# A fused attention and SwiGLU training step: dense heads in the weight and input products, four tail tiles taken among the last backward blocks, dy added in front of the row sums

## The chip, the cores and the metric

The kernel runs on one core of one Trainium2 chip. A core has TensorE (PE, with its weight loads listed as PEld), VectorE (DVE), ScalarE (ACT), GpSimd (POOL) and SyncE (SP), each with its own in-order queue; they wait for each other by semaphores. The metric is the device time of one execution in microseconds; the median of five runs is compared.

## The reference

The kernel computes the forward output and all six gradients of one layer: a layer norm, then attention and a SwiGLU block side by side, with a residual.

```python
S, D, H, F = 2048, 448, 16, 1792          # head size 28
xn = layernorm(x)                          # no scale, no offset
A  = softmax(q k^T * 28**-0.5) v @ wo      # q, k, v = xn @ wqkv, 16 heads
B  = (silu(xn @ w_gate) * (xn @ w_up)) @ w_down
out = x + A + B
# outputs: out, and by jax.vjp with grad_out: dx, dwqkv, dwo, dw_gate, dw_up, dw_down
```

All inputs and outputs are bf16. The last output to be finished is dx. With G the gradient at xn (a sum of the products from the SwiGLU block and from dq, dk and dv with wqkv transposed), the layer norm's backward is dx = dy + rstd * (G - mean(G) - xn * mean(G * xn)), row by row, so it needs two sums over each row of G.

## The kernel before, in words

**Heads and groups.** The 16 heads are worked in 4 groups of 4. A head has 28 columns; in SBUF each head takes 32 (HP), so that four heads fill 128 partitions and a matmul of one head can use a quarter of the array. The transposed gradients dq, dk and dv of a group are kept as 128 rows with 4 rows of padding per head: dkv (two tiles of 128 x 2048, one per head pair, each with two heads of dk and two of dv) and dqT.

**Forward.** 256 slots (slot, L598) each compute four score tiles and their exponentials; between them fillers run projections, the SwiGLU forward and backward and its weight gradients. load_wq (L209) loads the wqkv columns of a group, and POOL spreads them from 28 to 32 columns per head into wq_g. For the first group that happens at the very start, in front of the second identity matrix on POOL. store_wqT (L253) transposes wq_g by DMA and stores it to wqT_d with six DMAs for the end of the kernel.

**Backward.** NB = 512 steps: group, head pair, key chunk of 512, query chunk, query tile of 128. row (L804) puts the score and dP matmuls on PE into banks sb and db (three each), ew (L832) the exponential on ACT and the product ds on DVE. Four steps make a block: in it tr_unit (L892) transposes one ds tile on PE (the others go by DMA), kv (L904) accumulates dk and dv, and dq_unit (L936) dq. Each lags behind the rows, so after step 512 there are blocks without rows in which only these run. At the end of a key chunk, kv stores a slice of dkv to dqkvT_d; at the end of a head pair dq_unit stores dqT. Stores go through a list and are issued on POOL some steps later (store and flush, L795 and L799).

**Fillers of the backward loop.** A stream of units is cut into pieces that run between the parts of a block, one bank (genb) for all: fill_step stops when its room, measured against each unit's own estimate in ns, is used up; the last slot of a block finishes the unit. In order: the forward output (y_unit), the SwiGLU part of dx (dx_unit, 10 or 8 matmuls), then after tail_open (L1143) dc_unit (L1165), which adds dq, dk and dv of the first three groups times the transposed weights to dxg, nine matmuls of 128 rows for each of 16 tiles. Among them, once per group, dsp_unit and dsq_unit transpose dk, dv and dq back, and dwq_unit (L1007) forms the gradient of wqkv: 16 matmuls of 384 columns for each of four slices of D. The padding columns are left out when its result is cast.

**The tail.** After the loop, 16 tiles of 128 rows of dx are finished (L1294 to L1354). dx_a works a pair of tiles: PE adds the last group's products into a bank tok; for the tiles in EVEN, DVE adds them to dxg and sums the row in the same instruction (L1319); for the others PE adds dxg by an fp32 identity matmul and ACT takes the row sum (L1316). A second DVE instruction forms the sum with xn (L1322). dx_b works a tile later: DVE scales the two sums (L1329), ACT forms rstd * G minus the mean (L1332), DVE xn times its sum plus dy (L1335), and POOL (for the last tile DVE) adds the two (L1337) and SP stores. Between the pairs PE and DVE or ACT finish the last group's dwqkv (the list rest).

Of the kernel before, what the change touches and what calls it, by code (L numbers as in the profile page):

```python
# [16 lines left out]
S = 2048  # L17
D = 448
# [7 lines left out]
P = 128  # L26
SCALE = DH ** -0.5
# [6 lines left out]
EVEN = (0, 2, 4, 6, 7, 8, 9, 10, 11, 12)  # L34
# [69 lines left out]
def kernel(  # L104
# [37 lines left out]
    wqT_d = dram.tile([P, 3 * G, DP_], BF16)  # L142
    dqkvT_d = dram.tile([3 * G, P, S], BF16)
# [65 lines left out]
    def load_wq(g, eng):  # L209

        raw = wk.tile([P, 4, 3, 4 * DH], BF16, name="wraw", bufs=1)
# [6 lines left out]
        for c, (d0, dn) in enumerate(DCH):  # L218
            yield
            if c == 2 and g == 0:  # L220
                ln_rstd(0)
            r4 = raw[:dn, c].rearrange("p t (h d) -> p t h d", d=DH)
            w4 = wq[:dn, c].rearrange("p t (h r) -> p t h r", r=HP)
            POOL.tensor_copy(out=w4[:, 0:2, :, :DH], in_=r4[:, 0:2])
            POOL.tensor_copy(out=w4[:, 2, 0:2, :DH], in_=r4[:, 2, 2:4])
            POOL.tensor_copy(out=w4[:, 2, 2:4, :DH], in_=r4[:, 2, 0:2])

# [16 lines left out]
    wq_g, wq_gen = {}, {}  # L244
# [7 lines left out]

    def store_wqT(g):  # L253
        wT = wk.tile([P, 4, 3, P], BF16, name="wqT_st", bufs=1)
        w = wT[:].rearrange("p c t d -> p (c t) d")
        sp_transpose(w, wq_g[g][:].rearrange("p c t r -> p (c t r)"))
        for lo, tq, i in ((0, 0, 0), (64, 0, 0), (0, 1, 1), (64, 2, 1), (0, 2, 2), (64, 1, 2)):
            late.append((wqT_d[lo:lo + 64, 3 * g + i, :].rearrange("p (c d) -> p c d", c=4),
                         wT[lo:lo + 64, :, tq, :]))
# [539 lines left out]
    def flush(upto):  # L799
        while held and held[0][0] <= upto:  # L800
            _, o, i = held.pop(0)
            POOL.dma_start(out=o, in_=i)
# [101 lines left out]
    def kv(k):  # L904
# [16 lines left out]
        if last:  # L921
# [5 lines left out]
            if g < G - 1:  # L927
                ksl = slice(kc * 512, (kc + 1) * 512)
                store(dqkvT_d[3 * g + 1 + hp, :, ksl], dkv[g, hp][:, ksl])
# [6 lines left out]
    def dq_unit(b):  # L936
# [27 lines left out]
        if qc == 3:  # L964
            dst = dqkvT_d[3 * g].rearrange("r (a q s) -> r a q s", q=2, s=P)
            for par in range(2):
                store(dst[64 * hp:64 * hp + 64, :, par],
                      dqT[g][64 * par:64 * par + 64, hp].rearrange("r (a s) -> r a s", s=P))
            if hp == 1:
# [4 lines left out]
                stream[at:at] = [(2590, lambda c=c: dwq_unit(g, c)) for c in range(4)]  # L974

    def dsq_unit(g, hp, tag="genb"):
# [5 lines left out]
        DVE.tensor_copy(out=dsp[g][:, :, 0, 64 * hp:64 * hp + 64],  # L982
# [6 lines left out]
    def dsp_unit(g, kind, t8, tag="genb"):  # L989
# [11 lines left out]
        (ACTE.copy if tag == "rest" and t8 else DVE.tensor_copy)(out=dsp[g][:, 8 * t8:8 * t8 + 8, kind, :], in_=ps[:])  # L1001
# [5 lines left out]
    def dwq_unit(g, c, tag="genb"):  # L1007
        d0, dn = DCH[c]
        ps = (ps_b if tag == "rest" else ps_g).tile([P, 3 * P], FP32, name=tag, bufs=2 if tag == "rest" else 1)
        for t in range(NT):  # L1010
            PE.matmul(ps[:dn, :], lhsT=xn_sp[:, t, d0:d0 + dn], rhs=dsp[g][:, t].rearrange("p k r -> p (k r)"),
                      start=(t == 0), stop=(t == NT - 1))
            if t < NT - 1:
                yield 162
        o = bk.tile([P, 3, 4, DH], BF16, name="dwq_o")
        p4 = ps[:].rearrange("p (k h r) -> p k h r", k=3, r=HP)
# [8 lines left out]
        yield 162  # L1025
# [117 lines left out]
    def tail_open():  # L1143
        dxst.close()
        tw = dxs["tw"] = tlst.enter_context(tc.tile_pool(name="tw", bufs=2, reuse_waits="tile"))
        dxs["wq"] = tw.tile([P, 3 * G, D], BF16, name="wqT", bufs=1)
        drip(("dc", 0), [(dxs["wq"][:, a:a + 3, :], wqT_d[:, a:a + 3, :D]) for a in (0, 3, 6)], now + 15)
# [3 lines left out]
        for lo in (0, 64):  # L1151
            for hp in range(2):
                drip(("dc", 3), [(dxs["wqd"][lo:lo + 64, hp, :], wqT_d[64 * hp:64 * hp + 64, 3 * G - 3, :D])], NB - 20)
        drip(("dc", 3), [(dxs["wq"][:, 10:12, :], wqT_d[:, 10:12, :D])], NB - 20)
# [5 lines left out]
    def load_dc(ch):  # L1160
        dcs[ch] = dxs["tw"].tile([P, 3 * G - 3, 512], BF16, name="dc")
        drip(("dc", ch), [(dcs[ch][:, a:a + 3], dqkvT_d[a:a + 3, :, ch * 512:(ch + 1) * 512].rearrange("i p s -> p i s"))
                          for a in (0, 3, 6)], now + 16)

    def dc_unit(t):  # L1165
# [5 lines left out]
        for i in range(3 * G - 3):  # L1171
            PE.matmul(ps[:, :D], lhsT=dcs[t // 4][:, i, (t % 4) * P:(t % 4 + 1) * P], rhs=dxs["wq"][:, i, :],
                      start=(i == 0), stop=(i == 3 * G - 4))
            if i < 3 * G - 4:
# [17 lines left out]
    for t in range(NT):  # L1192
        stream.append((189 * 9, lambda t=t: dc_unit(t)))
# [25 lines left out]
    def fill_step(room):  # L1219
# [7 lines left out]
        cur = None  # L1227

    NEXT = [(1, 0), (1, 2), (3, 1), (3, 2)]
    kv_n = 0  # L1230
    for k in range(NB + 12):
# [29 lines left out]
        elif m == 1:  # L1261
            b = (k - 13) // 4
            if 0 <= b < NB // 4:
                dq_unit(b)
        elif m == 2:
# [5 lines left out]
    while stream:  # L1271
        for _ in stream.pop(0)[1]():
            pass

# [6 lines left out]
    tw, wqT = dxs["tw"], dxs["wq"]  # L1281
# [4 lines left out]
    psd, sms = {}, {}  # L1286

    g = G - 1
    both = [(dkv[g, 0], wqT[:, 3 * g + 1]), (dkv[g, 1], wqT[:, 3 * g + 2])]

    nrs = tw.tile([P, NT], FP32, name="nrs", bufs=1)
    POOL.tensor_scalar(out=nrs[:], in0=rstd[:], scalar1=-1.0 / D, scalar2=None, op0=ALU.mult)

    def dx_a(t0):  # L1294
        sm = sms[t0] = tw.tile([P, 2, 2], FP32, name="sm", bufs=4)
        for t in (t0, t0 + 1):
            pst = ps_b.tile([P, 512], FP32, name="tok", bufs=6)
            psd[t] = pst[:, :D]
        odd = [t for t in (t0, t0 + 1) if t not in EVEN]
        for t in (t0, t0 + 1):  # L1300
            for i, (l, r) in enumerate(both):
                PE.matmul(psd[t], lhsT=l[:, t * P:(t + 1) * P], rhs=r, start=(i == 0), stop=False,
                          skip_group_check=True)
            if t in odd:
# [80 lines left out]
```

The softmax here doesn't subtract the row's maximum and nothing guards it: scores larger than these inputs give would overflow.

## Time and profile before

Five runs: 1442.64, 1442.90, 1444.32, 1444.69 and 1445.22 us. The profiled execution took 1442.64 us.

| | us |
|---|---|
| median of the runs | 1444.32 |
| the profiled execution | 1442.64 |
| its span, first to last instruction | 1440.9 |
| forward, up to the first ds (start to 615.8) | 615.8 |
| backward blocks, up to the last ds of the loop | to about 1394 |
| from there to the end | about 47 |
| granted TensorE clock, mean | 0.986 |

Backward blocks of four steps, by what fills them (from the start of a block's first ds to the next):

| filling | matmuls of the unit | us per block |
|---|---|---|
| dx_unit, second third of F | 8 | 5.63 |
| dx_unit, last third | 10 | 5.69 |
| dc_unit | 9 | 5.63 |
| dwq_unit | 16 | 6.42, at the end of a key chunk up to 6.89 |

How to read the views: a window line gives the busy time of PE, PEld, DVE, ACT and POOL with the number of instructions in brackets, then the granted TensorE clock, the DMA engines' busy share and GB/s. A timeline line gives start, duration, engine, source line, operation, tiles out<-in, sizes and count, and in square brackets how long the engine stood idle before it and what ended that. In a listing by form, after the bar stand busy time, mean ns of one, and the idle time before them.

### The profile page before, as it was taken

The page shows a single profiled execution, that of the slowest core. Times are in us where ns is not written, and L with a number is a line of the kernel's source. Part 1 is how long each engine was busy: PE and PEld are TensorE (multiplying, and loading weights), DVE is VectorE, ACT ScalarE, POOL GpSimd, SP SyncE. Part 2 cuts the span into 40 slices and gives each one's busy share as a digit, 9 for nine tenths or more (in the row PEclk, how much of TensorE's full clock was granted, in tenths as well). Part 3 has the DMA queues.
Part 4 walks back from the last instruction along what each step waited for, and adds up shares of the span by engine and source line. Part 5 has one row for each costly group of instructions (what it writes and reads, how often), then busy time and mean ns, then how long its engine had stood idle before and what let it go on. Part 6 is the DMA issues. An engine that isn't in the chain of part 4 may idle for free. (4 is left out here: it accounts for less than half of the span.)

```text
span 1440.9 us, 34682 instructions
## 1 busy us (share of the span) xinstructions
PE 1328.2 (92%) x12647; PEld 541.1 (38%) x12708; DVE 1151.5 (80%) x1997; ACT 1261.1 (88%) x2193; POOL 405.9 (28%) x561
## 2 busy tenths in 40 slices
PE   5889999989999999889999989999999999999996
PEld 2333333333333333333333434433443344444343
DVE  6677757666677676588998989888989999989988
ACT  5789988988999999778988989899989999989974
POOL 6574514453344453111111112201111011010106
PEclk9999999999999999989999999999999999999998
DMA  5797857796678586799999999999999999999961
GB/s 153 177 203 179 217 129 170 175 203 155 156 163 193 141 177 137 190 226 223 218 216 216 224 210 190 213 215 231 226 169 201 203 218 216 214 195 207 192 139 60
DMA packets 681179, 271.69 MB, mean 189 GB/s; under 512 B 606424, under 2 KB 655824, under 8 KB 681008
## 3 DMA queue, kind: packets, MB, share of 16 engines
q1 hardware_dynamic: 672576, 255.35, 87.1%
q0 software_dynamic: 7024, 13.82, 4.1%
q8 instruction: 100, 1.64, 0.5%
q14 instruction: 71, 0.58, 0.1%
q10 hardware_dynamic: 1408, 0.30, 0.1%
HBM read 65.09 MB, written 60.36 MB: 87 GB/s over the span
## 5 line engine op out<-in xcount | busy, mean ns | idle before, releaser
L842 DVE TENSOR_TENSOR ds_sb<-db,e_sb 128x512 bf16<-128x512 f32 x1024 | 646.8, 684 | 53.8 <-issue 20.1
L836 ACT ACTIVATE e_sb<-sb 128x512 bf16<-128x512 f32 x1024 | 554.2, 610 | 60.2 <-PE db L820 44.2
L612 ACT ACTIVATE eT<-s_w 128x1024 bf16<-128x1024 f32 x256 | 263.6, 1030 | 45.9 <-PE s_ps L609 43.1
L614 ACT ACTIVATE eT<-s_ps 128x512 bf16<-128x512 f32 x512 | 280.0, 611 | 0.0
L820 PE MATMUL db<-kd,qd 32*128 32x512 bf16 x1024 | 235.9, 383 | 8.4 <-DVE ds_sb L842 7.5
L812 PE MATMUL sb<-kd,qd 32*128 32x512 bf16 x1024 | 210.1, 386 | 5.0 <-DMA qd<-QD_d 3.2
L961 POOL TENSOR_TENSOR dq_acc<-dq_acc,dq_st 128x256 f32<-128x256 f32 x64 | 46.3, 723 | 457.1 <-ACT dq_st L959 457.1
L919 PE MATMUL acc<-ds_sb,qd 128*32 128x512 bf16 x1024 | 160.0, 388 | 0.0
L915 PE MATMUL acc<-e_sb,qd 128*32 128x512 bf16 x1024 | 157.8, 389 | 1.4 <-DVE dw_o L528 1.4
L902 ACT COPY dsT<-db 128x1024 bf16<-128x1024 bf16 x128 | 130.0, 1016 | 14.7 <-PE db L897 14.0
L380 POOL TENSOR_TENSOR nn<-nn,ag 128x512 f32<-128x512 f32 x56 | 71.3, 1273 | 249.3 <-DVE ag L378 240.6
L609 PE MATMUL s_ps<-QQ,KK 32*128 32x512 bf16 x512 | 125.3, 384 | 4.0
L1128 PE MATMUL genb<-wguT,dau_c 128*128 128x448 bf16 x448 | 117.5, 355 | 6.3 <-ACT dq_st L959 3.9
L609 PE MATMUL s_w<-QQ,KK 32*128 32x512 bf16 x512 | 100.1, 386 | 13.2 <-ACT eT L612 10.3
L812 PEld LDWEIGHTS <-qd 32*128 32x128 bf16 x1024 | 48.2, 91 | 149.1 <-issue 139.6
L421 PE MATMUL gen<-xn_t,f_sp 128*128 128x448 bf16 x416 | 91.8, 354 | 2.6 <-DVE nn L395 1.7
L421 PEld LDWEIGHTS <-f_sp 128*128 128x128 bf16 x640 | 55.7, 98 | 75.7 <-issue 32.1
L946 PE MATMUL genb<-dsT,kd 128*32 128x256 bf16 x2048 | 79.7, 276 | 2.2 <-DVE dqT L955 0.6
L897 PE MATMUL db<-ident_bf,ds_sb 128*128 128x128 bf16 x1032 | 79.4, 220 | 1.1 <-DVE ds_sb L842 1.1
L897 PEld LDWEIGHTS <-ds_sb 128*128 128x128 bf16 x1032 | 68.2, 99 | 24.5 <-issue 5.6
L381 POOL TENSOR_TENSOR nn<-nn,tt 128x512 f32<-128x512 f32 x56 | 72.1, 1288 | 4.4
L609 PEld LDWEIGHTS <-KK 32*128 32x128 bf16 x1024 | 29.0, 91 | 115.3 <-issue 112.3
(167 smaller groups left out, 1953.2 us busy)
## 6 DMA issues: line engine op xcount, KB each, us to landing
F_d<-hda SPq DMA_DIRECT2D x56, 384.0 KB, 3.1
dau_c<-F_d SPq DMA_DIRECT2D x24, 512.0 KB, 4.4
qd<-QD_d SPq DMA_DIRECT2D x16, 512.0 KB
kd<-KD_d SPq DMA_DIRECT2D x16, 384.0 KB, 3.9
dsT<-ds_sb SPq DMA_TRANSPOSE x383, 4.5
dc<-dqkvT_d SPq DMA_DIRECT2D x12, 384.0 KB, 3.7
h_c<-F_d SPq DMA_DIRECT2D x8, 512.0 KB, 5.3
wT_d<-wT_f SPq DMA_DIRECT2D x14, 256.0 KB, 3.6
```

The costliest lines, as they stand in the source:

```text
L421: PE.matmul(ps[:, :D], lhsT=fsp[fc][:, t // 4, w, t % 4, :], rhs=rhs[:, t, :], start=(t == 0), stop=(t == NT - 1))
L609: PE.matmul(sp4[hh], lhsT=KK[g][r:r + HP, kt * P:(kt + 1) * P], rhs=QQ[g][r:r + HP, qsl], start=True, stop=True, tile_position=(r, 0))
L612: ACTE.activation(out=e2[0][:], in_=wide[:], func=ACT.Exp, scale=SCALE)
L614: ACTE.activation(out=e2[1][:, j], in_=sp4[2 + j], func=ACT.Exp, scale=SCALE)
L812: PE.matmul(s_ps[:], lhsT=qside[g, qc][r:r + HP, 0, qi * P:(qi + 1) * P], rhs=kside[g, kc][r:r + HP, 0, :], start=True, stop=True, tile_po ...
L820: PE.matmul(d_ps[:], lhsT=qside[g, qc][r:r + HP, 1, qi * P:(qi + 1) * P], rhs=kside[g, kc][r:r + HP, 1, :], start=True, stop=True, tile_po ...
L836: ACTE.activation(out=est[k][:, j], in_=sps.pop((k, j))[:], func=ACT.Exp, scale=SCALE)
L842: DVE.tensor_tensor(out=ds[:, j], in0=dps.pop((k - 1, j))[:], in1=est[k - 1][:, j], op=ALU.mult)
L897: PE.transpose(ps[:, c, :], ds[:, c // 4, (c % 4) * P:(c % 4 + 1) * P], ident_bf[:])
L902: ACTE.copy(out=o, in_=ps[:])
L915: PE.matmul(a[r:r + HP, :], lhsT=sp4[:, 1, r:r + HP], rhs=e[:, j, :], start=first, stop=last, tile_position=(0, r), skip_group_check=True)
L919: PE.matmul(a[r:r + HP, :], lhsT=sp4[:, 0, r:r + HP], rhs=ds[:, j, :], start=first, stop=last, tile_position=(0, r), skip_group_check=True)
```

## The change

It has five parts; lines that only rename are left out.

1. **Dense rows for dc_unit.** dq, dk and dv of the first three groups are stored without the padding rows, 1008 rows as 8 x 126 (crow gives each head's place), and the transposed weights come from the loaded columns themselves, which are padded with zeros to a multiple of 128. dc_unit has eight matmuls over 126 rows for nine over 128. dk and dv are stored once per head pair, in four DMAs of 28 rows, dq in four per head pair instead of two.
2. **Dense columns for dwq_unit.** 12 x 28 = 336 columns instead of 384; the moving operand skips the padding by its access pattern.
3. **Four tail tiles early.** The matmuls of tiles 0 and 1 stand behind dq_unit of block 125, their sums behind dq_unit of block 126, with the matmuls of tiles 2 and 3; they use the banks sb and db. The last stores after the loop go out on SP instead of POOL.
4. **dy in front of the sums.** For each tile DVE forms v = rstd * G + dy in dx_a, before the scaling of the sums; ACT forms u = xn * sum + sum, and dx = u + v.
5. **Who does what.** Tiles 1, 3 and 5 join EVEN; three copies of the last group move from DVE to ACT; the order of the remaining units of the last group changes; the last pair keeps its two sums in separate tiles.

```diff
@@ load_wq, store_wqT
-        raw = wk.tile([P, 4, 3, 4 * DH], BF16, name="wraw", bufs=1)
+        rawp = raws[g] = wk.tile([P, 4, 3 * P], BF16, name="wraw", bufs=1)
+        raw = rawp[:, :, :12 * DH].rearrange("p c (t n) -> p c t n", t=3)
...
+        POOL.memset(rawp[:, :, 12 * DH:], 0.0)
+        POOL.memset(rawp[64:, 3, :12 * DH], 0.0)
...
+        if g < G - 1:
+            sp_transpose(w, raws[g][:].rearrange("p c r -> p (c r)"))
+            for t in range(3):
+                a, n = 336 * g + P * t, min(P, 336 - P * t)
+                late.append((wqc_d[a:a + n, :].rearrange("p (c d) -> p c d", c=4), wT[:n, :, t, :]))
+            return
@@ flush
-            POOL.dma_start(out=o, in_=i)
+            (POOL if now < NB else SP).dma_start(out=o, in_=i)
@@ kv, dq_unit
-            if g < G - 1:
-                ksl = slice(kc * 512, (kc + 1) * 512)
-                store(dqkvT_d[3 * g + 1 + hp, :, ksl], dkv[g, hp][:, ksl])
+            if kc == 3 and g < G - 1:
+                for h in range(4):
+                    store(dqkvc_d[crow(g, 1 + hp, h), :], dkv[g, hp][HP * h:HP * h + DH, :])
...
+            for j in range(2):
+                dst = dqkvc_d[crow(g, 0, 2 * hp + j), :].rearrange("r (a q s) -> r a q s", q=2, s=P)
+                for par in range(2):
+                    r = 64 * par + HP * j
+                    store(dst[:, :, par], dqT[g][r:r + DH, hp].rearrange("r (a s) -> r a s", s=P))
@@ dwq_unit
-            PE.matmul(ps[:dn, :], lhsT=xn_sp[:, t, d0:d0 + dn], rhs=dsp[g][:, t].rearrange("p k r -> p (k r)"),
+            PE.matmul(ps[:dn].rearrange("p (a r) -> p a r", r=DH), lhsT=xn_sp[:, t, d0:d0 + dn], rhs=dsp[g][:, t].rearrange("p k (h r) -> p (k h) r", r=HP)[:, :, :DH],
...
-                yield 162
+                yield 142
@@ tail_open, load_dc, dc_unit
+        nrs = dxs["nrs"] = tw.tile([P, NT], FP32, name="nrs", bufs=1)
+        POOL.tensor_scalar(out=nrs[:], in0=rstd[:], scalar1=-1.0 / D, scalar2=None, op0=ALU.mult)
...
+        drip(("dc", ch), [(dcs[ch][:CP, a:b], src[:, a:b]) for a, b in ((0, 3), (3, 6), (6, 8))], now + 16)
...
-        for i in range(3 * G - 3):
+        for i in range(NCP):
@@ the tail, new
+    def dx_v(t):
+        ps = psd.pop(t)
+        vs[t] = kq.tile([P, 512], FP32, name="ds_sb", bufs=10)[:, :D]
...
+        DVE.scalar_tensor_tensor(out=vs[t], in0=ps, scalar=rstd[:, t:t + 1], in1=dy, op0=ALU.mult, op1=ALU.add)
...
+    def dx_a(t0):
...
+        if t0 == NT - 2:
+            dx_sm(t0)
+        for t in (t0, t0 + 1):
+            dx_v(t)
+        if t0 < NT - 2:
+            dx_sm(t0)
+
+    def dx_b(t):
+        sa, sb = sums(t, 0), sums(t, 1)
+        u = kq.tile([P, 512], FP32, name="e_sb", bufs=5)[:, :D]
+        ACTE.activation(out=u, in_=xn_sp[:, t, :], func=ACT.Identity, scale=sb, bias=sa)
+        dx = dxs["tw"].tile([P, D], BF16, name="dx", bufs=4)
+        (DVE if t == NT - 1 else POOL).tensor_tensor(out=dx[:], in0=u, in1=vs.pop(t), op=ALU.add)
+        SP.dma_start(out=out1_d[:, t, :], in_=dx[:])
@@ the loop, behind dq_unit
+            if k > NB and k < NB + 8:
...
+                if k < NB + 4:
+                    dx_mm(0)
+                else:
+                    dx_a(0)
+                    dx_mm(2)
@@ after the loop
+    ahead.update((t, tok(t)) for t in (4, 5))
+    for _ in range(4):
+        run(rest.pop(0))
+    dx_a(2)
+    at = {4: 1, 6: 1, 8: 1, 14: 1}
+    for t in range(4, NT + 2, 2):
         if t < NT:
+            dx_mm(t)
             dx_a(t)
-        for u in (t - 2, t - 1):
-            if u >= 0:
-                dx_b(u)
+        for u in range(0 if t == 4 else t - 2, t):
+            dx_b(u)
         for _ in range(at.get(t, 0)):
             run(rest.pop(0))
```

dx_mm holds the matmuls that dx_a began with before, in the same order; dx_sm is the scaling of the sums that stood in dx_b, and dx_a's row sums are unchanged. EVEN grows from (0, 2, 4, 6 to 12) to (0 to 12).

## The prediction

> **What bounds the kernel now.** I read the page's busy shares first, then busy times by window over blocks of four backward steps, then the timeline of one block and of the end.
>
> ```profile
> PE 1328.2 (92%) x12647; PEld 541.1 (38%) x12708; DVE 1151.5 (80%) x1997; ACT 1261.1 (88%) x2193; POOL 405.9 (28%) x561
> ...
> 1270.20:1276.60 6.40, 6.40 (x80) 2.85 (x76) 5.65 (x13) 5.51 (x11) 1.39 (x2) 1.00 1.07 215
> 1098.99:1104.62 5.63, 5.59 (x68) 2.17 (x69) 5.47 (x11) 5.39 (x12) 0.73 (x1) 1.00 0.99 214
> 1169.35:1175.04 5.69, 5.69 (x74) 2.34 (x67) 5.53 (x11) 5.43 (x11) 0.72 (x1) 1.00 1.08 244
> 1336.98:1342.61 5.63, 5.63 (x69) 2.24 (x69) 5.48 (x11) 5.38 (x12) 0.00 (x0) 1.00 1.17 247
> ```
>
> Three engines are nearly full, so the block decides. The windows are one block each, by the filling in them: dwq_unit (16 matmuls), dx_unit with 8, dx_unit with 10, dc_unit with 9. Eight and nine matmuls take the same 5.63 us, because VectorE is full; ten take 5.69. The dwq block takes 6.40, and there VectorE waits:
>
> ```profile
> 1267.13 0.39 PE L812 MATMUL sb<-kd,qd 32*128 32x512 bf16 x2
> ...
> 1267.50 0.50 PE L1011 MATMUL genb<-dsp,xn_t 128*128 128x384 bf16 x2
> ...
> 1268.28 1.30 PE L1011 MATMUL genb<-dsp,xn_t 128*128 128x384 bf16 x7
> ...
> 1269.51 0.39 PE L812 MATMUL sb<-kd,qd 32*128 32x512 bf16 x2
> ...
> 1269.62 0.27 DVE L1018 CAST dwq_o<-genb 128x112 bf16<-128x112 f32 x1 [0.65 <-PE genb L1011]
> ```
>
> Only the slot with nine of the sixteen matmuls (2 and 7) keeps VectorE waiting. The rows of scores ahead of it start just as VectorE frees a db bank (ds operations of about 0.64 us from 1263.82, rows at 1264.51, 1265.89, 1267.13), so the other seven lie in slack.
>
> The end:
>
> ```profile
> 1398.19 0.42 DVE L955 SCALAR_TENSOR_TENSOR dqT<-genb,dq_acc 128x256 bf16<-128x256 f32 x1 [0.80 <-PE genb L946]
> ...
> 1401.42 0.62 DVE L1319 SCALAR_TENSOR_TENSOR dxg<-tok,dxg 128x448 f32<-128x448 f32 x1 [1.59 <-PE tok L1309]
> ...
> 1433.33 1.08 DVE L1329 TENSOR_TENSOR sm<-sm,nrs 128x4 f32<-128x4 f32 x1
> 1434.52 2.04 DVE L1335 SCALAR_TENSOR_TENSOR ds_sb<-xn_t,sm,dsT 128x448 f32<-128x448 bf16 x2
> ...
> 1436.75 1.28 DVE L1337 TENSOR_TENSOR dx<-e_sb,ds_sb 128x448 bf16<-128x448 f32 x1 [0.19 <-issue]
> ```
>
> From 1401.42 to 1438.03 VectorE sets the pace with few gaps. By window it is busy only 4.75 of the 8 us before 1399. The listing by form shows whom the adds on POOL cost:
>
> ```profile
> L1322 DVE SCALAR_TENSOR_TENSOR pr<-dxg,xn_t 128x448 bf16<-128x448 f32 x10 | 8.3, 826 | 0.3
> ...
> L1322 DVE SCALAR_TENSOR_TENSOR pr<-tok,xn_t 128x448 bf16<-128x448 f32 x6 | 3.6, 618 | 0.7 <-ACT gs L1316 0.7
> ```
>
> **Dense heads.** *dwq_unit:* 336 columns for 384. Spacing of the seven matmuls is (1.30 - 0.326) / 6 = 0.162 us; by columns 0.142. Nine in the deciding slot save 9 x 0.020 = 0.18; the split becomes 2, 5, 3 and 6 under the new estimates, so again nine. Twelve units lie in the loop: **-2.2 us**. Ends: 0 if another wait takes over at once, and 16 x 0.020 x 12 = -3.9 if all count (VectorE's idle time there, 8.4 us over twelve, in the view of its line, would allow it). I take nine, since the timeline shows which are covered. The four units in the tail lie beside VectorE: 0; uncovered they would gain 4 x 16 x 0.020 = 1.3.
>
> *dc_unit:* eight matmuls for nine, 16 times. The windows say 0: VectorE covers them. Without that cover the gain would be 16 x 0.19 = 3.0.
>
> *Stores of dq, dk, dv:* POOL issues 24 of 28 rows x 4 KB for 24 of 128 KB (0.57 us each), and 24 for 12 of dqT (0.70). That is 12 x 0.70 = 8.4 us more of issuing, in batches of four: 2.3 or 2.8 us. POOL idles about 5 us in each block before its add of dq (L961, 457 us in all), which hides a batch; a y store behind one is 2.8 us late, while y has two buffers and a new one comes each 5.9 us. Uncovered, the 8.4 us would stand in full. SP issues 9 fewer stores of the transposed weights in the forward loop; the 12 dc loads stay 12 and land in 3.7 us, due 16 steps (22 us) ahead: 0.
>
> The Trainium skill, DMA: Bandwidth & Descriptors, in the section on why a DMA increments its semaphore by 16, says that a transfer is spread over the largest number up to 16 that divides its slowest dimension. By that, 126 or 28 rows use 14 engines, and a dc load of 3.7 us would land in an estimated 4.2, which moves no sum; no run here shows it yet.
>
> *load_wq:* two more memsets on POOL. Rows of 128x128 take 0.205 and 64x256 0.307, so about 0.25 and 0.35. In the first group they stand before ident_f, in a stretch where POOL is busy without a break from 9.04 to rstd at 15.64, for which VectorE waits 0.56 (L238 at 16.72); from there VectorE is full until the next projection on PE. **+0.5 us**, ends 0 and +0.65. For the other three groups POOL waits 240 us on the gates: 0.
>
> **The tail.** PE takes dx_mm(0), eight matmuls or about 1.3 us (L1302 x4 and L1309 x4), ahead of tr_unit(127) and dq_unit(126), and dx_mm(2) ahead of dq_unit(127). VectorE takes dx_a(0), seven operations, ahead of the last L955, and dx_a(2) behind it. No dx store moves ahead of the two dy loads on SP. Against the tail as it ran:
>
> - Start: L955 of dq_unit(126) ends at 1398.6 + 1.3 = 1399.9, and the first dx operation follows at once, for 1401.42: -1.5.
> - Three copies (L1001 0.69, L982 1.28 for two) go to ACT: -2.0. ACT takes four copies of 1.01 while VectorE does the first four tiles.
> - The last L955 now stands in the stretch: +0.4. Behind it wait genb, hence one rest bank, dsq and the dwq units; PE still has tile 4 ready by about 1407.4, before VectorE wants it at 1407.9.
> - Tiles 1, 3 and 5 gain a sum operation: 3 x 0.67 (1401.42 to 1402.09) = +2.0; tile 5's pr then reads SBUF beside the adds, +0.3. Six fp32 matmuls on PE go, beside VectorE.
> - Waits that go: 0.54 and 0.78 on tok, 0.67 on ACT's gs: -2.0.
> - v (new place of the L1335 work) now stands before the sums, so POOL's adds, 2.4 to 2.8 us a pair, fall on pr and on v instead of on a PSUM sum. Two v's took 1.28 alone and 2.04 beside adds. I take +0.3 for five pairs: +1.5; ends 0 and 0.6.
> - Last pair: from sm of tile 12 with the two pr's it took 7.2, less 1.28 for v12 and v13, which move = 5.9. After: ACT does two u (1.47), four casts (0.6), two u (1.4), then the 1.28 add: 4.8. -1.1.
>
> - nrs (0.27 us on POOL) moves to tail_open and waits there for the tiles of the dx pool; the next in POOL's queue is an add of dq that needs later PE work anyway: 0, and 0.3 if not. The four last dwq stores leave POOL (0.69 each, between its adds) for SP, where each waits for ACT's casts with the following dx stores behind it; the casts end before those dx tiles do: 0, or about 0.4 (one issue of SP) ahead of the last two.
>
> Sum **-2.4 us**. Ends: -4.7 if the adds cost v nothing and VectorE, not ACT, ends the last pair (0.8 sooner); +0.6 if the start gains nothing and v pays double.
>
> Total -2.2 + 0.5 - 2.4 = **-4.1 us**: the profiled execution of 1442.64 (span 1440.9, 1.7 outside it) becomes 1438.5, its span 1436.8. It was the fastest of the five; from the median 1444.32 I predict **1440.2**. Ends: 1435.7 and 1445.6.
>
> **Rivals.** (1) The dwq blocks find another wait as the dc blocks did: -1.9, 1442.4. For it: ACT is busy 5.51 of 6.40. Against: VectorE's idle 0.65 comes before its casts, straight after PE.
> (2) Both gains at their full ends, with the 0.5: -8.1, 1436.2. For it: the idle 8.4 us and a last pair free of POOL; against: the rows gated by db.
> (3) The end is held by ACT and POOL, tail 0: -1.7, 1442.6. For it: casts before the last two u's; against: POOL is busy 22 of 39 us there.
> (4) Slower: dwq's moving operand is now read in runs of 28 out of 32 elements, and no matmul of the trace reads such short runs. Nearest slow row is the fp32 matmul of 448 columns, spaced 0.92 - 0.54 = 0.38 us against 0.19 for bf16. At that rate a dwq matmul takes 0.285: 9 x 0.123 x 12 = +13.3, less 1.9: 1455.7, and 1466 if all sixteen count. It turns the sum positive from 0.162 + 1.9 / 108 = 0.180 us a matmul.
> The Trainium skill, SBUF — State Buffer, Door 1 (the DMA port swizzle), puts free striding at two or more accesses in each 16-byte line; a run of 56 bytes on a 64-byte grid keeps that, so by it rival 4 falls away. No row here shows it.
>
> **How the numbers follow.** Forecast 0.50 (own range 1438 to 1442.5), rivals 0.14, 0.18, 0.08, 0.10. Measurement tells about 0.2%, 2.9 us, from no change. Faster: most of the forecast (0.42), rival 2, a little of 1 and 3: 0.63. Slower: rival 4 and a remainder: 0.12. Same: 0.25. Range 1436 to 1444.5: rival 4 and the far tips stay out.
>
> **What would show it.** dwq blocks at 6.2 us with VectorE's wait near 0.47, and matmuls spaced 0.142; dc blocks still 5.63; first sum of tile 0 near 1399.9 - 1.7 = 1398.2; no wait before the sum of tile 4; v beside adds over 0.9 us; KK's second projection 0.5 us later at the start. A dwq spacing over 0.18 or a tail of 36 us again would make it wrong.

## The result, and the profile after

The changed kernel took 1445.17 us (median of 43 runs, 1438.93 to 1452.02), the kernel before, run beside it, 1442.90 (79 runs, 1437.29 to 1451.83). The ratio is 1.0014, 95% interval 1.0006 to 1.0023: some 2.0 us slower (0.0014 x 1443; 0.9 to 3.3), where 4.1 us less were predicted. Both kernels spread over more than 10 us, so that one profile is one draw: the profiled execution before had a span of 1440.9, the one after 1446.3.

The first view is the busy time by window over four stretches: forward, blocks 0 to 39, blocks 40 to 127, and from the last block on. The columns are start:end, length, busy PE, PEld, DVE, ACT, POOL, then the granted clock, the DMA share and GB/s. Before:

```profile
8.02:616.38 608.36, 557.04 (x3997) 215.32 (x4059) 402.70 (x709) 534.05 (x831) 272.54 (x360) 0.99 0.75 172
616.38:864.42 248.04, 229.99 (x2545) 93.93 (x2547) 222.00 (x366) 218.13 (x404) 38.36 (x62) 0.97 1.11 216
864.42:1389.01 524.59, 504.52 (x5816) 212.94 (x5817) 481.29 (x816) 484.32 (x906) 69.02 (x103) 1.00 1.09 204
1389.01:1440.90 51.89, 36.65 (x298) 18.91 (x294) 40.73 (x94) 23.34 (x55) 22.15 (x19) 0.88 0.31 83
```

The same stretches after:

```profile
8.00:620.77 612.77, 560.73 (x3998) 216.63 (x4060) 403.75 (x711) 534.55 (x831) 274.56 (x368) 0.98 0.73 171
620.77:869.20 248.43, 229.22 (x2545) 93.82 (x2547) 222.56 (x366) 218.52 (x403) 39.91 (x65) 0.97 1.12 216
869.20:1395.60 526.40, 502.36 (x5800) 211.99 (x5802) 480.81 (x815) 485.32 (x905) 73.87 (x112) 1.00 1.11 201
1395.60:1446.30 50.70, 33.23 (x292) 17.72 (x292) 43.01 (x98) 24.56 (x52) 19.64 (x15) 0.87 0.34 85
```

The first stretch ends with the first ds, which begins at 616.38 us before (not at 615.8). Of the 5.4 us between the spans, 4.4 arise in the forward loop, where the change adds two memsets a group and leaves out nine stores of weights. The blocks from the 40th on, which should have got 2.2 us shorter, took 1.8 more. The end got 1.2 shorter.

The 1.8 us are a sum of opposite parts. The twelve dwq blocks got 2.9 us shorter. Blocks 97 to 101 took 2.6 us more at a full clock, with waits of 1.4 us on a load of qd and 1.2 us on transposes of ds; the other profiles with rows stored in batches (e3, e10 and e11 below) lack this. Block 110, the first with a dc_unit, took 1.4 more, and two later dc blocks 0.35 each.

Single blocks after, in the same view: dx_unit with 8 matmuls, with 10, two with dwq_unit, two with dc_unit (blocks 114 and 115):

```profile
1096.18:1101.81 5.63, 5.58 (x68) 2.17 (x69) 5.47 (x11) 5.38 (x12) 0.73 (x1) 1.00 1.11 174
1172.18:1177.87 5.69, 5.69 (x74) 2.34 (x67) 5.52 (x11) 5.43 (x11) 0.73 (x1) 1.00 1.15 216
1269.27:1275.46 6.19, 6.19 (x80) 2.75 (x72) 5.62 (x13) 5.70 (x11) 1.00 (x2) 1.00 1.18 158
1275.46:1281.66 6.20, 6.20 (x78) 2.84 (x76) 5.63 (x13) 5.63 (x11) 1.46 (x2) 1.00 1.03 201
1319.57:1325.63 6.06, 5.83 (x68) 2.26 (x69) 5.74 (x12) 5.50 (x11) 0.00 (x0) 1.00 1.06 239
1325.63:1331.26 5.63, 5.59 (x68) 2.17 (x70) 5.47 (x10) 5.10 (x10) 0.00 (x0) 1.00 1.35 179
```

The dwq blocks take 6.20 as predicted. The dc blocks take 5.63, but one in this fence (block 114) and one more later (block 122) took 0.35 longer (6.06 for 5.71, 5.98 for 5.63). PE's part of the timeline of one dwq block:

```profile
1271.63 0.89 PE L1028 MATMUL genb<-dsp,xn_t 128*128 128x336 bf16 x5
...
1272.91 0.60 PE L1028 MATMUL genb<-dsp,xn_t 128*128 128x336 bf16 x3
...
1273.79 1.02 PE L1028 MATMUL genb<-dsp,xn_t 128*128 128x336 bf16 x6
```

Six matmuls are spaced (1.02 - 0.305) / 5 = 0.143 us, 0.305 being the length of one. By columns 0.142 were worked out, so the short runs of 28 elements cost nothing here.

The start, in POOL's timeline:

```profile
10.69 0.25 POOL L231 MEMSET wraw<- 128x192 bf16 x1
11.00 0.37 POOL L232 MEMSET wraw<- 64x336 bf16 x1
...
16.37 1.05 POOL L237 TENSOR_TENSOR rstd<-rstd,m_half 128x4 f32<-128x4 f32 x1
```

rstd stood at 15.64 before: +0.73.

The end, in DVE's timeline:

```profile
1405.03 0.61 DVE L1311 SCALAR_TENSOR_TENSOR dxg<-sb,dxg 128x448 f32<-128x448 f32 x1
...
1411.47 1.28 DVE L1288 SCALAR_TENSOR_TENSOR ds_sb<-dxg,rstd,dy 128x448 f32<-128x448 f32 x2
...
1413.74 0.63 DVE L1311 SCALAR_TENSOR_TENSOR dxg<-tok,dxg 128x448 f32<-128x448 f32 x1 [0.92 <-PE tok L1279]
...
1417.13 3.02 DVE L1288 SCALAR_TENSOR_TENSOR ds_sb<-dxg,rstd,dsT 128x448 f32<-128x448 f32 x2
...
1420.14 0.61 DVE L1311 SCALAR_TENSOR_TENSOR dxg<-tok,dxg 128x448 f32<-128x448 f32 x1
1420.79 0.62 DVE L1314 SCALAR_TENSOR_TENSOR pr<-dxg,xn_t 128x448 bf16<-128x448 f32 x1
...
1422.83 2.14 DVE L1288 SCALAR_TENSOR_TENSOR ds_sb<-dxg,rstd,dsT 128x448 f32<-128x448 f32 x2
...
1424.96 0.61 DVE L1311 SCALAR_TENSOR_TENSOR dxg<-tok,dxg 128x448 f32<-128x448 f32 x1
```

and in POOL's:

```profile
1414.10 5.56 POOL L1328 TENSOR_TENSOR dx<-e_sb,ds_sb 128x448 bf16<-128x448 f32 x4 [21.87 <-ACT e_sb L1326]
1421.20 2.68 POOL L1328 TENSOR_TENSOR dx<-e_sb,ds_sb 128x448 bf16<-128x448 f32 x2 [1.54 <-DVE dxg L1311]
```

Two v's take 1.28 us alone, 2.14 beside the adds of one pair, and 3.02 beside the four adds of the early tiles, which all come at once behind pair 4. A pair takes 4.82 (1420.14 to 1424.96), against 4.35 before (1417.25 to 1421.60):

```profile
1417.25 0.62 DVE L1319 SCALAR_TENSOR_TENSOR dxg<-tok,dxg 128x448 f32<-128x448 f32 x1
...
1421.60 0.62 DVE L1319 SCALAR_TENSOR_TENSOR dxg<-tok,dxg 128x448 f32<-128x448 f32 x1
```

Tile 4 is waited for 0.92 us. PE's transposes ahead of it wait 2.17 us for the last dq, and then run at half speed, for the clock is at 0.50 from 1409.1 to 1412.5. The same eight transposes, first after and then in e2 below: there the clock is full, PE waits as long, and VectorE does not wait for tile 4 at all:

```profile
1409.19 1.01 PE L1015 MATMUL rest<-ident_bf,dkv 128*128 128x128 bf16 x8 [2.17 <-DVE dqT L971]
1397.94 0.61 PE L998 MATMUL rest<-ident_bf,dkv 128*128 128x128 bf16 x8 [2.16 <-DVE dqT L955]
```

Last, the clock. Windows of one us at one place of the forward loop, after:

```profile
182.00:183.00 1.00, 0.25 (x2) 0.16 (x2) 1.00 (x3) 0.99 (x3) 0.15 (x1) 1.00 0.69 151
183.00:184.00 1.00, 1.00 (x6) 0.46 (x5) 0.22 (x1) 0.00 (x0) 0.47 (x1) 0.84 0.51 111
184.00:185.00 1.00, 1.00 (x7) 0.22 (x5) 0.00 (x0) 0.00 (x0) 0.00 (x0) 0.50 0.23 86
185.00:186.00 1.00, 1.00 (x7) 0.33 (x7) 0.00 (x0) 0.35 (x1) 0.00 (x0) 0.50 1.01 253
```

and the same place before, one us earlier in its span:

```profile
181.00:182.00 1.00, 0.69 (x4) 0.38 (x4) 0.79 (x2) 0.91 (x2) 0.58 (x1) 1.00 0.96 219
182.00:183.00 1.00, 1.00 (x10) 0.38 (x7) 0.00 (x0) 0.00 (x0) 0.04 (x1) 1.00 1.17 214
183.00:184.00 1.00, 1.00 (x8) 0.42 (x9) 0.00 (x0) 0.59 (x1) 0.00 (x0) 1.00 0.48 87
```

Behind a stretch in which PE stands idle (1.72 us after, 1.37 before) the granted clock falls to 0.50 for 3.4 us after and stays at 1.00 before, and what follows on the path is late by about 1 us. After has such falls at 184 and 314 us, and longer ones than before at 20 and 40; the shift of the forward slots between the two profiles grows at these places (by 1.4 and 0.95 us at the first two). The Trainium skill, TensorE: Matmul & The Clock Gate, in Part 1, says that PE runs at half rate after an idle window of 3.4 us and that the window runs free of the kernel's start. The trace agrees on the half rate (0.50 or 1.00, and means of the two where a window of the table holds both) and on the length and the free running: in both profiles the changes of the clock lie whole multiples of 3.41 us apart. It differs on the idle time: in the 3.4 us ahead of the fall at 183.7 PE was busy for half of the time and idle for 1.72 us at a stretch, so less than a whole idle window was enough. Since the windows run free, the same idle stretch can bring a fall in one execution and none in the next.

Every run lists its mean granted clock. It was 0.9791 in the changed kernel (44 executions) and 0.9822 to 0.9825 in the kernel before (means of 29 to 35 executions on each of four chips). Within the runs of the kernel before the time falls by 0.59 to 0.96 us for each 0.001 of clock, by chip (correlation -0.49 to -0.79), within the changed kernel's by 0.77 (-0.62). So 0.0032 less goes with 1.9 to 3.1 us, 2.5 by the changed kernel's own slope. This is a correlation: no run changes the clock and nothing else.

### The profile page after: what moved, and what is told of

Same layout as the page of the kernel before. It is cut to its first block, busy times and chain, and to the rows that moved or that the text cites. A ratio compares the mean times of both kernels' runs of the same rounds, so it can differ in the third digit from the quotient of the medians.

```text
span 1446.3 us, 34642 instructions
## 1 busy us (share of the span) xinstructions
PE 1325.5 (92%) x12625; PEld 540.1 (37%) x12686; DVE 1154.7 (80%) x2001; ACT 1264.2 (87%) x2190; POOL 411.8 (28%) x577
## 5 line engine op out<-in xcount | busy, mean ns | idle before, releaser
L836 PE MATMUL db<-kd,qd 32*128 32x512 bf16 x1024 | 239.8, 384 | 9.8 <-DVE ds_sb L858 8.5
```

What stands on the lines that cost most here:

```text
L836: PE.matmul(d_ps[:], lhsT=qside[g, qc][r:r + HP, 1, qi * P:(qi + 1) * P], rhs=kside[g, kc][r:r + HP, 1, :], start=True, stop=True, tile_po ...
```

## The experiments

In the traces the blocks from the 40th on repeat to 0.02 us from kernel to kernel (the dwq blocks of e1 and of the changed kernel, for instance), except where the clock falls or a transfer is late, so that small steps can be read there even where a ratio can't tell.

**Each part alone, and one taken away.** *e1_dwq*: only the dense dwq_unit.

```diff
-            PE.matmul(ps[:dn, :], ..., rhs=dsp[g][:, t].rearrange("p k r -> p (k r)"),
+            PE.matmul(ps[:dn].rearrange("p (a r) -> p a r", r=DH), ..., rhs=dsp[g][:, t].rearrange("p k (h r) -> p (k h) r", r=HP)[:, :, :DH],
```

> The kernel before with the dense dwq_unit alone (336 columns for 384). Theory rows (the dense rows of dq, dk, dv and of the weights cost about 5 us in the loop and the start, and eat a dwq gain of 2.9 and a tail gain of 1.2): 2.9 us less, ratio 0.998. Rival tail (the dwq gain is 2.9, the rows cost under 1, and the new tail is some 4 us slower than it looks): also 0.998. Rival slack (the dwq blocks get shorter but the loop gets it back elsewhere): ratio 1.000.

Ratio 0.9984 (0.9966 to 1.0002); clock 0.9825. From the start of block 40 to that of block 127 it took 521.65 us for 524.59: -2.94, all of it in the twelve dwq blocks, of which one by window:

```profile
1271.17:1277.36 6.19, 6.19 (x76) 2.84 (x76) 5.62 (x13) 5.62 (x11) 1.39 (x2) 1.00 1.06 240
```

No other of these blocks differs by more than 0.02 us, so nothing gives it back there: the rival of the slack falls.

*e2_norows*: the changed kernel with part 1 undone.

```diff
-            if kc == 3 and g < G - 1:
-                for h in range(4):
-                    store(dqkvc_d[crow(g, 1 + hp, h), :], dkv[g, hp][HP * h:HP * h + DH, :])
+            if g < G - 1:
+                ksl = slice(kc * 512, (kc + 1) * 512)
+                store(dqkvT_d[3 * g + 1 + hp, :, ksl], dkv[g, hp][:, ksl])
...
-        for i in range(NCP):
+        for i in range(3 * G - 3):
```

> The changed kernel with the dense rows undone (dq, dk, dv and weights in blocks of 128 rows again, nine matmuls in dc_unit, no two memsets); dense dwq_unit and the new tail stay. Theory rows: 2.9 + 1.2 = 4.1 us less than before, ratio 0.997, and no waits on the transposes of ds after a group's end. Rival tail: 1.1 us more, ratio 1.001. Rival slack: about 1.001, since neither dwq nor the tail pays.

0.9984 (0.9964 to 1.0004), clock 0.9818. Its point lies 0.0030 below the changed kernel, so the rows cost something, but between the two theories' numbers. The long dc blocks are gone (5.71 and 5.63).

*e3_rows*: only part 1, on the kernel before.

```diff
+            if kc == 3 and g < G - 1:
+                for h in range(4):
+                    store(dqkvc_d[crow(g, 1 + hp, h), :], dkv[g, hp][HP * h:HP * h + DH, :])
...
+        POOL.memset(rawp[:, :, 12 * DH:], 0.0)
+        POOL.memset(rawp[64:, 3, :12 * DH], 0.0)
```

> The kernel before with the dense rows alone (stores by heads of 28 rows in batches of four, eight dc matmuls, two memsets). Theory rows: 4 to 6 us more, ratio 1.0028 to 1.004, of it 0.75 at the start and the rest in the blocks after the batches of stores and at the first dc_unit. Rivals tail and slack: 0.5 to 0.8 us more, ratio 1.0005.

1.0006 (0.9987 to 1.0025), clock 0.9828: the rivals' 1.0005 fits, and the theory's 1.0028 to 1.004 lies outside, if barely. In its trace rstd stands at 16.48 and the dc blocks of 6.06 and 5.98 are there: 0.75 and 0.7 us that belong to the rows. Two more blocks (48 and 64), each with the one behind it, lose 1.2 and 1.1 us; see e8 and e9 on these.

*e4_tail*: only the new tail.

```diff
+                if k < NB + 4:
+                    dx_mm(0)
+                else:
+                    dx_a(0)
+                    dx_mm(2)
...
+        for t in (t0, t0 + 1):
+            dx_v(t)
```

> The kernel before with the new tail alone (early tiles, v ahead of the row sums, three copies on ScalarE, last stores on SP). Theory rows: 1.2 us less, ratio 0.999. Rival tail: 3 to 4 us more, ratio 1.0025. Rival slack: about 1.001.

0.9993 (0.9974 to 1.0012), clock 0.9829: the rival of a slow tail, 1.0025, falls. From its first sum to the end of its last add it takes 37.90 us against 36.60 before. Its first sum comes 4.91 us behind the start of the last ds. Before it was 7.90 in the profile, but 6.45 in e3, which has the old tail; the new tail has 4.91 here and 6.26 in e2. The clock parts them: before and in e2 it falls to 0.50 right behind the last ds (at 1394.0 before), in e3 and here it does not. One us of the stretch before and one of that in e3:

```profile
1395.00:1396.00 1.00, 1.00 (x17) 0.57 (x10) 0.19 (x1) 0.57 (x1) 0.00 (x0) 0.50 0.00 0
1399.00:1400.00 1.00, 1.00 (x29) 0.89 (x27) 0.94 (x2) 0.25 (x1) 0.00 (x0) 1.00 0.13 15
```

All 17 profiles go by this: with a fall there the first sum comes 7.85 to 7.90 us behind the last ds in the old tail and 6.21 to 6.33 in the new one, without it 6.45 and 4.90 to 4.91. So like with like the first sum gains 1.5 us, as predicted. The stretch from it to the last add gives back 0.9 to 1.5, and the last store lands 0.2 to 0.3 later. From the last ds to the end of the span it is 46.76 us in e2 for 47.34 before, with the fall, and 45.86 here for 45.78 in e3 without it: the tail is worth nothing, or a gain of half a us. Where the new tail has no fall right behind the last ds, one comes some 9 us later, at the wait ahead of tile 4.

**Mending the rows.** *e5_mend*: the changed kernel with the stores of a batch three steps apart, the first group's memsets behind the start, and the first dc loads four steps earlier.

```diff
-    def store(o, i):
-        held.append((now + 2, o, i))
+    def store(o, i, lag=2):
+        held.append((now + lag, o, i))
+        held.sort(key=lambda x: x[0])
...
-                    store(dqkvc_d[crow(g, 1 + hp, h), :], dkv[g, hp][HP * h:HP * h + DH, :])
+                    store(dqkvc_d[crow(g, 1 + hp, h), :], dkv[g, hp][HP * h:HP * h + DH, :], 2 + 3 * h)
...
-        POOL.memset(rawp[:, :, 12 * DH:], 0.0)
-        POOL.memset(rawp[64:, 3, :12 * DH], 0.0)
+        if g:
+            pad_wq(g)
...
-... for a, b in ((0, 3), (3, 6), (6, 8))], now + 16)
+... for a, b in ((0, 3), (3, 6), (6, 8))], now + (16 if ch else 12))
```

> The changed kernel with three mends of the dense rows: the four stores of a batch are let go three steps apart instead of together, the two memsets of the first group stand behind the start, and the first loads of dc fall due four steps earlier. Theory batch (a burst of four row stores holds up the transposes of ds that VectorE's operations wait for, and the first dc load comes too late): the blocks after a group's end and the first dc block lose their 1 to 4 us of waits, the blocks from the 40th on take 522.4 us as a whole against 526.4 changed and 524.6 before, the start loses 0.75, and the ratio to before is 0.998. Rival form (rows of 28 cost DMA time however they are issued): only the start and the dc block gain, 2.1 of some 5 us, ratio 1.000. Rival luck (the waits come and go between runs): ratio as the changed kernel's less 0.0005, 1.001.

0.9971 (0.9954 to 0.9988), clock 0.9807: faster than both kernels. Its profile is one of its longer executions (1442.70 us) and has 523.9 us from block 40 on where 522.4 were expected; the clock falls at blocks 64 and 96 and takes 2.2 of them; the two long dc blocks are gone. Run again on another chip as *e15_mend2*:

> The mended kernel of the fifth experiment once more, unchanged, on the chip of these runs. If its gain was the kernel's, ratio to before 0.996 to 0.999; if it was that chip's or chance, 0.999 to 1.001, as the sum of its traced parts plus the changed kernel's lower clock would make it.

0.9982 (0.9965 to 1.0000), clock 0.9802. The gain holds, if smaller: its interval ends at 1.

The three mends one by one, each on the changed kernel. *e9_spread* has only the `lag`, *e10_dcearly* only `now + (16 if ch else 12)` (and 11 for 15 at the weights), *e11_memset* only `pad_wq`.

> The changed kernel with only the four row stores of a batch let go three steps apart. Theory batch: it brings the part of the mended kernel's gain that the start and the dc loads don't explain, some 3 us of 6: ratio to before 0.9993, blocks 97 to 101 at before's times. Rival late (the dc loads and the start are the systematic cost, and waits after a group's end come by chance in every kernel): ratio as the changed kernel's, 1.001, with the waits at the first dc block and the two long dc blocks (6.06 and 5.98 us) still there.

> The changed kernel with only the first loads of dc and of the dense weights due four steps earlier. Theory late: the first dc block loses its wait (1.4 us) and the two long dc blocks are 5.7 and 5.63 us (0.7 less together): 2.1 us less, ratio to before 1.000. Theory batch: the same 2.1 us here, and the rest in the other experiment. Rival: earlier loads push transposes of ds aside, and the dwq blocks before get longer by what the dc block gains: ratio 1.0014.

> The changed kernel with only the two memsets of the first group moved behind the start. All theories: GpSimd's second rstd begins at 15.6 to 15.9 instead of 16.37, and the forward slots come 0.75 us earlier: ratio to before 1.0009. If the start is hidden after all: 1.0014.

0.9996 (0.9981 to 1.0012), 1.0003 (0.9991 to 1.0015) and 0.9996 (0.9978 to 1.0013): each below 1.0014, none apart from it. In the traces: the memsets' 0.73 us go in e11 (rstd at 15.75). The dc blocks of 6.06 and 5.98 stay in e10 and e11 and are gone in e9, e5 and e15 (5.71 and 5.63), so they hang on the stores going in a batch, by a way that the profile doesn't name: the last store of dq, dk or dv is issued at 1224.5, some 95 us ahead. The wait for the first dc loads, 1.4 us after, in the view of waits by window

```profile
PEld L1192 <- DMA dc<-dqkvc_d: 1.7, 1, 1.7
PE genb L1192 <- DMA dc<-dqkvc_d: 1.4, 1, 1.4
```

is gone in e10, but also in e11 and e3, and 0.35 of it is left in e9: it shows only where SyncE's queue happens to be late. After, the last piece was issued at 1293.15 and the unit's first matmul began at 1296.28, 3.1 us later; before at 1285.05 and 1291.77, 6.7 us. PE wanted that piece for its seventh matmul at 1298.54 and had it at 1299.93, 6.8 us behind the issue (6.2 in e9), where the loads before landed in 3.5 to 4.3. Whether the form of the rows or the queue made it slower isn't shown.

*e8_batch* batches the stores of the kernel before, with 128 rows as they were:

```diff
-            if g < G - 1:
-                ksl = slice(kc * 512, (kc + 1) * 512)
-                store(dqkvT_d[3 * g + 1 + hp, :, ksl], dkv[g, hp][:, ksl])
+            if kc == 3 and g < G - 1:
+                for c in range(4):
+                    ksl = slice(c * 512, (c + 1) * 512)
+                    store(dqkvT_d[3 * g + 1 + hp, :, ksl], dkv[g, hp][:, ksl])
```

> The kernel before with nothing but its four stores of a dk or dv held back to the end of the last key chunk and let go together: 128 rows as before, no dense row. Theory batch: waits of 1 to 3 us in the blocks after a group's end (blocks 48, 64 and 96 on), together 2 to 3 us, ratio 1.0015 to 1.002. Rival form: no such waits, ratio 1.000, blocks from the 40th on 524.6 as before.

1.0003 (0.9984 to 1.0022): no long blocks at 48, 64 or 96, but one at 80 (7.55 for 6.68). In e9 the blocks 64 and 96 are long in spite of the spread stores, and in e6 below, which has no dense rows, 48, 64 and 96. The clock tells why; e9 by windows, at block 64:

```profile
1019.00:1020.00 1.00, 0.24 (x1) 0.10 (x1) 1.00 (x3) 1.00 (x3) 0.00 (x0) 1.00 0.29 56
1020.00:1021.00 1.00, 0.94 (x10) 0.94 (x10) 1.00 (x3) 0.10 (x1) 0.00 (x0) 0.56 1.14 260
1021.00:1022.00 1.00, 1.00 (x13) 0.74 (x10) 0.27 (x2) 0.17 (x1) 0.00 (x0) 0.50 0.84 285
```

Here PE waits twice for the bank of the transposes, 0.89 and 0.82 us, in each of the 17 profiles; in eight of them the clock falls behind it and 0.9 to 1.2 us go. So the theory that a batch of stores holds up the transposes of ds falls for these blocks. Waits on those transposes there were in the changed kernel's profile, at blocks 32 to 34, right behind the batches of group 0, 4.1 us on DVE:

```profile
DVE ds_sb L858 <- DMA dsT<-ds_sb: 4.1, 3, 1.9
PE genb L962 <- DMA dsT<-ds_sb: 2.0, 2, 1.7
```

but blocks 30 to 38 are unsteady in kernels without rows too (7.60 for 5.88 at block 34 in e1).

**The tail.** *e6_adds*, on e2: the last steps of the early tiles ahead of pair 4.

```diff
+    dx_b(0)
+    dx_b(1)
     for _ in range(4):
         run(rest.pop(0))
     dx_a(2)
+    dx_b(2)
+    dx_b(3)
...
-        for u in range(0 if t == 4 else t - 2, t):
+        for u in range(4 if t == 4 else t - 2, t):
```

> The second experiment (no dense rows) with the last steps of tiles 0 to 3 put ahead of pair 4, so that GpSimd's first four adds run while VectorE does early tiles and waits, not beside pair 4's sums and v's. Theory v (v beside an add takes 1.54 us for 0.67): pair 4 falls from 6.4 to 4.8 us or less, and the stretch from the first sum to the end from 40.5 to about 39. Rival: ScalarE's steps for tiles 0 to 3 delay its four copies, dsp comes later and the end is the same or up to 2 us later. Ratio to before 0.9975 or 0.9985.

0.9975 (0.9958 to 0.9992). Pair 4 falls from 6.4 to 4.5 us with its v's at 1.28, but there is a wait of 1.61 before it, which e2 does not have:

```profile
1409.77 0.62 DVE L1293 SCALAR_TENSOR_TENSOR dxg<-tok,dxg 128x448 f32<-128x448 f32 x1 [1.61 <-PE tok L1261]
...
1413.01 1.28 DVE L1270 SCALAR_TENSOR_TENSOR ds_sb<-dxg,rstd,dsT 128x448 f32<-128x448 f32 x2
```

and the adds of tiles 0 and 1 now slow the v's of pair 2 (2.14). The stretch is 38.1 (37.45 in e2): the theory was right on pair 4, and on the end the rival's number came. But the clock is at 0.50 for 6.8 us around that wait, so how much of it the order makes and how much the clock isn't settled.

*e7_vback*, on e2: the last step as it was.

```diff
-        ACTE.activation(out=u, in_=xn_sp[:, t, :], func=ACT.Identity, scale=sb, bias=sa)
+        ACTE.activation(out=t1, in_=psd.pop(t), func=ACT.Identity, scale=rstd[:, t:t + 1], bias=sa)
+        DVE.scalar_tensor_tensor(out=t2, in0=xn_sp[:, t, :], scalar=sb, in1=dy, op0=ALU.mult, op1=ALU.add)
```

> The second experiment (no dense rows) with the last step of a tile in its old form: VectorE's second operation is xn times the sum plus dy again, behind the row sums, and ScalarE reads G; the early tiles stay. Theory v: pairs 6, 8 and 10 take 4.35 us again instead of 4.82, pair 4 also 4.4 to 5, the stretch from the first sum to the end is some 2 us shorter (38.5), less up to 1 us at the last pair. Rival (the extra sums of tiles 1, 3 and 5 and the waits are what costs): the stretch stays at 40 to 41.

0.9979 (0.9962 to 0.9997). The middle pairs take 4.35 us again, with 1.28 for the two operations; DVE's timeline from pair to pair:

```profile
1416.60 0.62 DVE L1285 SCALAR_TENSOR_TENSOR dxg<-tok,dxg 128x448 f32<-128x448 f32 x1
...
1419.76 1.27 DVE L1301 SCALAR_TENSOR_TENSOR ds_sb<-xn_t,sm,dsT 128x448 f32<-128x448 bf16 x2
1420.95 0.62 DVE L1285 SCALAR_TENSOR_TENSOR dxg<-tok,dxg 128x448 f32<-128x448 f32 x1
```

But pair 4, expected at 4.4 to 5, takes 6.78 us, for its four last operations stand beside adds too (4.23 for the four), and the last two tiles pay again (1.55 and 1.54). Tile 4 is waited for 1.02 us. The stretch is 38.0: these lose what the middle gains. The theory holds for v, not for the end.

*e12_tail2* and *e13_tail3*, on e5, mix both forms:

```diff
-        for t in (t0, t0 + 1):
-            dx_v(t)
+        if t0 >= 12:
+            for t in (t0, t0 + 1):
+                dx_v(t)
...
+    dx_mm(4)
+    dx_a(2)
+    dx_b(0)
+    dx_b(1)
     for _ in range(4):
         run(rest.pop(0))
```

and e13 besides

```diff
+            if t == 12:
+                dx_b(t - 2)
+                dx_b(t - 1)
             dx_a(t)
...
-        (DVE if t == NT - 1 else POOL).tensor_tensor(out=dx[:], ...)
+        (DVE if t in (NT - 3, NT - 1) else POOL).tensor_tensor(out=dx[:], ...)
```

> The mended kernel (fifth experiment) with another tail: v ahead of the sums only for the last four tiles, the old last step for the other twelve, tile 4's products on TensorE ahead of the transposes that wait for the last dq, and the last steps of tiles 0 and 1 ahead of ScalarE's copies. Theory v (v beside GpSimd's adds costs what the last pair gains): pairs of 4.35 us in the middle, no wait of 0.9 before tile 4, the last pair as in the changed kernel, stretch from the first sum to the last add 36 us instead of 38: ratio to before 0.996. Rival (some other engine, ScalarE or GpSimd, holds the tail at 38): ratio 0.997 as the mended kernel.

> The mended kernel with the tail of e12 and its two faults put right: the last steps of tiles 10 and 11 stand ahead of pair 12, and the add of tile 13 is on VectorE, so that GpSimd has not five adds left at the end. Theory v: middle pairs 4.35 us, last dx add some 36.5 us behind the first sum (38.1 in the changed kernel, 40 in e12), the tail from the last ds to the end 44.5 us where the first sum comes 4.9 us behind it (46.1 in the changed kernel); ratio to the mended kernel of the same chip 0.999. Rival (ScalarE or GpSimd hold the end whatever VectorE does): 38 again, ratio 1.000 to it.

e12: 0.9996 (0.9979 to 1.0013). Tile 6 comes late: DVE waits 5.62 us for it, behind a dwq unit whose 16 matmuls take 4.12 us for 2.45, as the clock falls there. Then POOL still has five adds left when DVE has done its last sums, and the end comes 48.3 us behind the last ds, 1.6 later than in e5; POOL's timeline:

```profile
1430.65 6.09 POOL L1343 TENSOR_TENSOR dx<-e_sb,ds_sb 128x448 bf16<-128x448 f32 x5 [1.97 <-DVE ds_sb L1341]
```

e13: 1.0011 (0.9996 to 1.0026), 50.3 us; against e15, beside which it ran, 1.0025 by the medians. Tile 6 comes late again, behind a dwq unit that waits for ACT's copies, after 6.8 us at half clock:

```profile
1417.53 0.62 DVE L1319 SCALAR_TENSOR_TENSOR dxg<-tok,dxg 128x448 f32<-128x448 f32 x1 [4.22 <-PE tok L1286]
```

Both miss: with DVE eased, POOL's adds and PE's order hold the end, with falls of the clock on top that the profiles don't let one take out. *e14_tail3n* has e13's tail without the rows:

> The same tail without the dense rows (on the second experiment). If the mended rows cost nothing, its ratio to before is that of e13_tail3 within 0.001; if rows of 28 cost DMA time however they are issued, it is 0.001 to 0.002 lower and its granted clock is higher.

1.0007 (0.9988 to 1.0026), clock 0.9798 against e13's 0.9782: the ratios are within 0.001, but their intervals leave room for 0.002 either way, and the clock is higher by about one error. So this does not tell what the mended rows cost.

## Why the prediction was wrong

It called the direction wrong. Its mechanisms in the loop were mostly right; two sizes (the new work of the tail and the stores) and one resource (the clock) were not.

- **dwq, -2.2.** Right: -2.94 in twelve blocks (e1), 6.20 a block, with a spacing of 0.143 in the changed kernel. The split was 2, 5, 3 and 6, as worked out; nine count, and a little more of the other seven. Rival 4 (short runs) is refuted, rival 1 too.
- **dc_unit, 0.** Right for 14 of 16 blocks; two lost 0.35 each while the stores came in batches. Its "due 16 steps (22 us) ahead: 0" was wrong as a margin: the last piece was issued only 3.1 us ahead of the unit, and landed in 6.8 us instead of 3.7, or 4.2 by the prediction's other estimate. One profile of those with batches shows 1.4 us of waiting, e9 0.35. The due step is where the plan aims, not where a full queue issues.
- **The stores, 0.** Issuing was indeed hidden by POOL: in the backward loop no other engine waits for it. What the stores did elsewhere was not costed. Undoing or mending part 1 together with its start is worth 0.0030 to 0.0043 of ratio (e2, e5 and e15 against the changed kernel), each with an interval of some 0.002 either way; of this 0.75 us at the start and 0.7 in the dc blocks are placed, the rest not.
- **load_wq, +0.5.** 0.73, just over its end of 0.65.
- **The tail, -2.4.** This is the step that failed by size. The first sum came 1.5 us sooner, as worked out, though the row that it was measured from, 1401.42, had a fall of the clock in front. "I take +0.3 for five pairs" for v beside POOL's adds was wrong. The prediction's own row, 2.04 for 1.28, made 0.76 a pair, and no reason was given for less than half of it. Three pairs pay 0.86 (2.14 for 1.28), pair 4, on which the adds of all four early tiles fall, 1.74, and tile 12 0.33: together 4.65 for 1.5. Cheaper pr's in three pairs (0.62 for 0.90) give back 0.8. "Tile 4 ready before VectorE wants it" held in e2 and e5 and failed (0.92) where the clock fell in front of it. Measured: -1.5 at the first sum, +0.9 to +1.5 in the stretch, +0.25 at the last store, so about 0. Rival 3 had a tail of 0, but for another reason, ACT and POOL holding the end.
- **The granted clock.** No step had it. The sum was made against a profile with 0.986 and carried to the median as if the clock were the kernel's own constant. It is not: the changed kernel has 0.0032 less on average, which goes with some 2.5 us.

Together -2.9 + 0.7 + 0.7 + 0 + 2.5 = +1.0, against +2.0 (0.9 to 3.3) measured. For e5 and e15 the same sum makes -2.9 + 0 + 1.2 = -1.7 and -2.9 + 0 + 1.8 = -1.1 (0.0015 and 0.0023 less clock than before on their chips), against -4.2 and -2.6 measured (intervals of 2.5 us each way); what is left there isn't settled. Nor is it settled which part lowers the clock. dwq, rows and tail alone left it (0.9825, 0.9828, 0.9829; 12 runs each, errors 0.0006 to 0.0010); dwq and tail together had 0.9818, 0.9803, 0.9818 and 0.9798, all three 0.9782 to 0.9817. No kernel was made that keeps PE busy at those places, which would be the test.

## What to carry to other kernels

Where a loop repeats, take the price of a step from the blocks and not from the total: here twelve blocks gave 2.94 us to the hundredth, while the total needed 43 runs to tell 2. Work that is moved beside a second engine's SBUF operations must be priced at the instruction it will stand beside, one by one, and the engine that is not the bound must be followed too: each mended tail found the next one (POOL's adds, PE's order). A step of preparation, such as a pad or a batch of stores, is best put where no one waits for its queue: moving them, with the loads a little earlier, stands between a loss of 2 us and a gain of 3 to 4, of which the traces place 1.5 us. And look at the granted clock of a window before its times are compared: here it parted two profiles of the same tail by 1.4 us.

## What the hardware showed that was not expected

The clock of PE falls to 0.50 for 3.4 us at fixed places of the program, behind idle stretches on PE where this was looked at (1.72 us in the forward loop; 0.89 and 0.82 us, 3.0 us apart, at a head pair's end), in one execution and not in the next. A fall costs 0.9 to 1.4 us on the path in the loops and 1.3 to 1.5 right behind the last ds. Outside the tail the clock was at 0.50 for 27.3 us before and 44.4 after in the two profiles, eight times 3.4 us and thirteen times: five more, beside 5.4 us more of span. Time and clock go together from run to run (correlation -0.4 to -0.9 in the kernels run), and so does a good part of the spread of 10 us. And two DVE operations on SBUF alone take 1.28 us, beside one pair of POOL adds 2.14, and beside back to back adds 3.02, while one that reads PSUM keeps its 0.61.
